# Moving the second GEMM's products one unit later in the pinned order of a fused attention and feed-forward kernel

## The chip, the cores and the metric

The kernel runs on one core of a Trainium2 chip. The metric is the device time of one execution in microseconds. Three runs of the kernel before took 962.63, 962.66 and 961.5 us, a median of 962.63 us.

## What is computed

The input is q, k and v of 8 batches, 8 heads, 576 positions and 64 channels, in float32. Two attentions are added: one over sequences shortened by a mean over four positions, and a local one in which each position sees itself and three neighbours on either side. The sum becomes the rows `x` of a feed-forward layer with 4608 rows, 512 inputs and 2048 hidden values:

```python
    x = np.ascontiguousarray(attn_out.transpose(0, 2, 1, 3)).reshape(B * S, H * D)
    h = x @ w_in
    r = np.maximum(h, 0.0)
    g = s * (r * r) + b
    return (g @ w_out).astype(np.float32)
```

## The kernel before

**Tiles.** The rows are cut into 18 tiles `t` of 256, the hidden values into 8 parts `p` of 256. A block is one pair (t, p); `order` lists the 144 blocks. From t = 3 on, where this study plays, the blocks come in plain order, eight to a row tile, so that block 8t + p is (t, p). To keep float32 precision every operand is split in a high and a low part (`xh`, `xl`, `gh`, `gl`), and each product is made of three matmuls.

**A block's work.** `products1` (L631) multiplies `w_in` with `x`: 24 matmuls of 256 columns into one PSUM bank `ph`. It yields after 3, 12 and 24 of them, so it is given out in parts of 3, 9 and 12. Then ScalarE works in place on `ph`: relu (L646) and square (L647), and casts it to `gh` (L648). VectorE subtracts `gh` from `ph` and writes `gl` (L653), after which the bank is free. `products2` (L712 to L714) multiplies `g` with `w_out`: four units of three matmuls of 512 columns, two units for the upper 128 rows (m = 0, into one bank `po`), two for the lower (m = 1, into another). The sums over the eight parts p stay in these two banks.

**Eviction.** With part p = 7 a row tile is done. After the second unit of that block `evict_half` (L686) scales the m = 0 bank into `os` on VectorE, after the fourth unit the m = 1 bank, and SyncE sends each with a DMA (L689). From t = 3 on all row tiles use the same two banks (0 and 1), so the next tile's first unit, which starts a new sum in bank 0, must wait until the m = 0 eviction has read it.

**Buffers.** Even blocks use bank 4 for `ph`, odd ones bank 6. There are three pairs of `gh` and `gl`, so the cast of block n must wait for the last unit of block n - 3.

**The order of the work.** An order written out by hand (`PLAN`) runs the first 28 blocks, with their w_out products, among the start of the attention. Behind it a loop takes two blocks at a time, `st` (even) and `st + 1`. In it `products("G", n)` gives out n parts of w_in's products and `products("H", n)` n units of w_out's, and every matmul of both is chained to the one before, so that TensorE meets them in exactly the order of the text. An iteration is: 3 products of block st, one unit, 21 products of block st, one unit, 24 products of block st + 1, six units. `finish` issues the relu, square, cast and subtraction of a block. In the iteration of st = 28 (`BEGIN`) no unit is given out, and the loop ends with eight units, so that the units trail: before the change the six units of an iteration are units 2 and 3 of block st - 2 and all four of block st - 1.

**The attention beside it.** `advance` and `split` issue steps of the attention of later batches and the split of the next row tile of `x` (L612, L613). The local attention multiplies q with shifted k on GpSimd (L537), sums on VectorE (L539), takes a softmax (L542 to L550), multiplies v by the weights on VectorE (L558) and adds on GpSimd or VectorE (L559). Its loads `lqk` and `lv` (L530, L532) go through SyncE's queue, as do those of the other attention (L154) and the stores of `os`. A scheduler with a simulated timeline places the attention's instructions on all engines, and the eviction, the subtraction and the casts with them. Each engine then runs its own list in order.

Of the kernel before, what the change touches and what calls it, by code (L numbers as in the profile page):

```python
# [20 lines left out]
B, H, S, D = 8, 8, 576, 64  # L21
# [65 lines left out]
def attention_ffn_kernel(ctx, tc, qk, vw_in, vr_in, vdm, qkn, vn, w_in, w_out, s_in, b_in, out):  # L87
# [706 lines left out]
    BEGIN = 28  # L794
# [66 lines left out]
    @contextlib.contextmanager  # L861
    def behind_plan():

        traced = nc.cur_bb.bb.instructions
        last = traced[-1]
        yield
        start = next(k for k in reversed(range(len(traced))) if traced[k] is last) + 1
        for i in traced[start:]:
            if i.engine in ENGINES:
                tc.add_manual_dep(  # L870
                    i, tail[i.engine].name,
                    mybir.DependencyInfo(
                        mybir.DependencyClass.NoSync, mybir.DependencyReason.DATA),
                    reason="behind_plan")
# [3 lines left out]
    def products(kind, count):  # L878

        nonlocal chain_end  # L880
        for _ in range(count):
            traced = nc.cur_bb.bb.instructions
            last = traced[-1]
            next(streams[kind])
            start = next(k for k in reversed(range(len(traced))) if traced[k] is last) + 1
            for i in traced[start:]:
                if i.engine == nc.tensor.engine:
                    tc.add_manual_dep(
                        i, chain_end.name,
                        mybir.DependencyInfo(  # L890
                            mybir.DependencyClass.NoSync, mybir.DependencyReason.DATA),
                        reason="products")
                    chain_end = i

    def finish(st):
        with tc.high_priority():
            next(streams["R"])
            next(streams["V"])
        advance(st + 0.5)
# [32 lines left out]
    def advance(st):  # L932
        nonlocal done
        while done < target(st):
            with tc.high_priority(offset=300 if done < NY[1] else 60 if done < NY[1] + NY[2] else 0):
                if next(gen, "end") == "end":
                    break
            done += 1
# [3 lines left out]
    def split(st):  # L942
        if order[st] in splits:
            split_x(splits[order[st]])

    for st in range(BEGIN, len(order), 2):
        begun = st > BEGIN
        with behind_plan() if st < BEGIN + 10 else contextlib.nullcontext():
            products("G", 1)
            products("H", 1 * begun)  # L950
            products("G", 2)
            finish(st)
            products("H", 1 * begun)
            advance(st + 1)
            split(st)
            products("G", 3)
            finish(st + 1)
            products("H", 6 * begun)
            advance(st + 2)
            split(st + 1)  # L960
    products("H", 8)


def _layout(q, k, v):
# [59 lines left out]
```

## Time and profile before

| | |
|---|---|
| median of three runs | 962.63 us (961.5 to 962.66) |
| profiled execution | 959.7 us |
| its span, first to last instruction | 957.9 us |
| TensorE busy | 924.6 us, 97% of the span |
| VectorE, ScalarE, GpSimd busy | 645.2, 478.2 and 412.9 us |
| granted TensorE clock, mean | 0.989 |

In the rows of the views PE is TensorE, PEld its weight loads, DVE VectorE, ACT ScalarE, POOL GpSimd, and SPq the queue of SyncE, which issues the DMAs. A row of the waits has the engine and line that waited, who ended the wait, and then microseconds in total, number of times and the longest. A row of the timeline has a start, a duration (from the first start to the last end where several instructions are merged, xN) and, in brackets, the idle time of the engine just before it and who ended it. A row of the chain has a start, a length and the work; consecutive matmuls stand there from start to start. A row of the windows has the stretch, its length, each engine's busy time and number of instructions, the granted clock, the busy share of the DMA engines and GB/s.

### The profile page before, as it was taken

To read this page: it belongs to the slowest core of one execution; us is meant where nothing else is said; L and a number is where in the kernel's file an instruction comes from. 1 tells how busy PE (TensorE), PEld (TensorE's weight loads), DVE (VectorE), ACT (ScalarE), POOL (GpSimd) and SP (SyncE) were. 2 spreads that over 40 slices of the span, in tenths; PEclk is the share of its full clock that TensorE was granted. 3 is DMA by queue.
4 is the path that set the end of the run, shared out by engine and by line. 5 is a ranking of instruction groups with operands and counts; after the bars stand their busy time and mean duration, and the time that the engine had idled before them with its cause. 6 is when DMAs were issued, how large, how long until landed. Compare 5 with 4: busy or idle time off the path is not lost.

```text
span 957.9 us, 18429 instructions
## 1 busy us (share of the span) xinstructions
PE 924.6 (97%) x7316; PEld 831.1 (87%) x7316; DVE 645.2 (67%) x1134; ACT 478.2 (50%) x1133; POOL 412.9 (43%) x440
## 2 busy tenths in 40 slices
PE   6699999999999999999999999999999999999998
PEld 5588888888889989898999899889898999999997
DVE  9999999844688879787878797787877421211121
ACT  7977775466553636354544454544434333332332
POOL 6401130010587776767676768676776200000000
PEclk9699999999999999999999999999999999999999
DMA  9755413223232323323232323232311000000000
GB/s 327 264 169 179 144 47 114 71 71 102 90 107 96 110 89 108 97 91 111 83 106 81 123 79 126 80 113 91 114 54 43 1 23 1 23 1 23 1 23 22
DMA packets 32022, 86.25 MB, mean 90 GB/s; under 512 B 3520, under 2 KB 8128, under 8 KB 31936
## 3 DMA queue, kind: packets, MB, share of 16 engines
q1 hardware_dynamic: 31936, 85.08, 27.2%
q8 instruction: 57, 0.93, 0.4%
q14 instruction: 29, 0.24, 0.1%
HBM read 75.63 MB, written 9.44 MB: 89 GB/s over the span
## 4 chain that ended last, share of the span: by engine, by line
PE 54%; DVE 18%; POOL 17%; issue 5%; ACT 3%; DMA 2%; DVEq 0%; POOLq 0%; ACTq 0%
PE ph L631 24%; PE po L712 8%; POOL pr L537 8%; PE po L713 8%; PE po L714 8%; POOL acc L559 6%; DVE pv L558 3%; DVE acc L559 2%; DVE gl L653 1%; DVE st L539 1%; DVE bias L669 1%; PE sa L342 1%; DMA lqk<-in_qkn_dram 1%; PE ol L479 1%; DVE es L272 1%
## 5 line engine op out<-in xcount | busy, mean ns | idle before, releaser
L631 PE MATMUL ph<-xh,wi 128*128 128x256 f32 x2176 | 414.0, 280 | 1.6 <-DVE gl L653 1.6
L631 PEld LDWEIGHTS ph<-xh,wi 128*128 128x128 f32 x2176 | 345.2, 189 | 10.7 <-DVE gl L653 2.7
L631 PE MATMUL ph<-xl,wi 128*128 128x256 f32 x1152 | 321.6, 279 | 0.0
L537 POOL TENSOR_TENSOR pr<-lqk 128x576 f32<-128x576 f32 x140 | 206.4, 1495 | 77.0 <-DMA lqk<-in_qkn_dram 53.7
L631 PEld LDWEIGHTS ph<-xl,wi 128*128 128x128 f32 x1152 | 217.4, 189 | 7.3 <-DVE xl L771 0.2
L646 ACT ACTIVATE ph<-ph 128x512 f32<-128x512 f32 x144 | 83.9, 582 | 235.1 <-PE ph L631 227.1
L712 PE MATMUL po<-wo,gh 128*128 128x512 f32 x416 | 166.3, 400 | 4.6 <-DVE os L686 4.5
L713 PE MATMUL po<-wo,gh 128*128 128x512 f32 x416 | 164.0, 394 | 0.0
L714 PE MATMUL po<-wo,gl 128*128 128x512 f32 x416 | 162.8, 391 | 0.8 <-DVE gl L653 0.7
L653 DVE TENSOR_TENSOR gl<-ph,gh 128x512 fp32r<-128x512 f32 x104 | 71.0, 683 | 105.4 <-ACT gh L648 105.0
L539 DVE TENSOR_REDUCE st<-pr 128x9 f32<-128x576 f32 x140 | 106.2, 759 | 48.4 <-POOL pr L537 45.9
L559 POOL TENSOR_TENSOR acc<-acc,pv 128x576 f32<-128x576 f32 x80 | 115.0, 1437 | 54.0 <-DVE pv L558 31.5
L558 DVE TENSOR_TENSOR pv<-lv,st 128x576 f32<-128x576 f32 x120 | 87.3, 745 | 32.4 <-POOL acc L559 32.1
L312 POOL TENSOR_TENSOR dq<-vt 80x64 f32<-80x64 f32 x58 | 20.7, 368 | 174.5 <-PE up L383 173.3
L714 PEld LDWEIGHTS po<-wo,gl 128*128 128x128 f32 x416 | 78.1, 188 | 18.9 <-DVE gl L653 2.1
L712 PEld LDWEIGHTS po<-wo,gh 128*128 128x128 f32 x416 | 78.1, 188 | 18.6 <-DVE os L686 4.4
L713 PEld LDWEIGHTS po<-wo,gh 128*128 128x128 f32 x416 | 78.3, 188 | 11.1 <-issue 0.2
L647 ACT ACTIVATE ph<-ph 128x512 f32<-128x512 f32 x144 | 83.8, 582 | 3.7
L712 PE MATMUL po<-wo,gb 128*128 128x512 f32 x160 | 63.3, 396 | 3.5 <-DVE os L686 3.5
L648 ACT CAST gh<-ph 128x512 fp32r<-128x512 f32 x104 | 61.0, 587 | 9.5 <-PE po L713 6.7
L653 DVE TENSOR_TENSOR gb<-ph,gb 128x512 fp32r<-128x512 f32 x40 | 27.3, 682 | 53.9 <-ACT gb L648 53.9
L713 PE MATMUL po<-wo,gb 128*128 128x512 f32 x160 | 62.9, 393 | 0.0
(158 smaller groups left out, 1243.2 us busy)
## 6 DMA issues: line engine op xcount, KB each, us to landing
tqk<-in_qk_dram SPq DMA_DIRECT2D x30, 584.0 KB, 3.7
lqk<-in_qkn_dram SPq DMA_DIRECT2D x20, 768.0 KB, 4.6
lv<-in_vn_dram SPq DMA_DIRECT2D x20, 480.0 KB, 3.3
out_dram<-os SPq DMA_DIRECT2D x34, 256.0 KB, 2.3
wst<-in_moe_w_in_dram SPq DMA_DIRECT2D x7, 1024.0 KB, 5.9
wst<-in_moe_w_out_dram SPq DMA_DIRECT2D x7, 1024.0 KB, 4.9
tvd<-in_vdm_dram SPq DMA_DIRECT2D x29, 160.0 KB, 2.4
tvr<-in_vr_dram SPq DMA_DIRECT2D x29, 128.0 KB, 2.2
```

Source lines behind the costliest of these rows:

```text
L537: nc.gpsimd.tensor_tensor(pr, lqk[:, 0:CH], lqk[:, CH + o : 2 * CH + o], ALU.mult)
L539: nc.vector.tensor_reduce(ls[:, :, o], pr, AX.X, ALU.add)
L558: nc.vector.tensor_tensor(pv, lv[:, o : o + CH], w, ALU.mult)
L559: (nc.vector if o % 3 == 1 else nc.gpsimd).tensor_tensor(acc[:, :, h], acc[:, :, h], pv, ALU.add)
L631: nc.tensor.matmul(ph[:, j], wi[p][:, s, k, f], xk[:, k], start=k == 0 and s == 0 and xk is xh, stop=k == NK - 1 and s == 1)
L646: nc.scalar.activation(ph, ph, AF.Relu)
L647: nc.scalar.activation(ph, ph, AF.Square)
L648: nc.scalar.copy(gh, ph)
L653: nc.vector.tensor_tensor(gl, acc.pop((t, p)), gh.bitcast(F32), ALU.subtract)
L712: nc.tensor.matmul(po[m], gh[:, j, ms], wo[p][:, 0, j], start=first, stop=False)
L713: nc.tensor.matmul(po[m], gh[:, j, ms], wo[p][:, 1, j], start=False, stop=False)
L714: nc.tensor.matmul(po[m], gl[:, j, ms], wo[p][:, 0, j], start=False, stop=last)
```

## The change

One unit of w_out's products less is given out ahead of the 21 products in the iteration of st = 30, the first that gives out any, and one more behind the loop. From then on the stream of units is one unit later against the text of the loop: the unit ahead of the 21 products is the fourth of the block before, the unit behind them the first of block st - 2, and the six behind block st + 1 are units 1, 2 and 3 of block st - 2 and units 0, 1 and 2 of block st - 1. At the end of a row tile the fourth unit of its last block, and the m = 1 eviction that is issued with it, move from the end of one iteration into the next, and the first unit of the next row tile moves from in front of the 21 products to behind them. The number of products and of every other instruction is the same.

```diff
@@ -947,7 +947,7 @@
         begun = st > BEGIN
         with behind_plan() if st < BEGIN + 10 else contextlib.nullcontext():
             products("G", 1)
-            products("H", 1 * begun)
+            products("H", 1 * (st > BEGIN + 2))
             products("G", 2)
             finish(st)
             products("H", 1 * begun)
@@ -958,7 +958,7 @@
             products("H", 6 * begun)
             advance(st + 2)
             split(st + 1)
-    products("H", 8)
+    products("H", 9)
```

## The prediction

> **What bounds the kernel now.** I read the page first, for the engine that fills the span, and then the busy time by stage.
>
> ```profile
> span 957.9 us, 18429 instructions
> PE 924.6 (97%) x7316; PEld 831.1 (87%) x7316; DVE 645.2 (67%) x1134; ACT 478.2 (50%) x1133; POOL 412.9 (43%) x440
> PE 54%; DVE 18%; POOL 17%; issue 5%; ACT 3%; DMA 2%; DVEq 0%; POOLq 0%; ACTq 0%
> 262.00:742.00 480.00, 470.88 (x3184) 428.35 (x3184) 383.66 (x684) 229.10 (x587) 346.64 (x321) 1.00 0.30 96
> 742.00:957.00 215.00, 212.08 (x1381) 192.05 (x1379) 45.60 (x69) 69.79 (x119) 5.75 (x4) 1.00 0.04 13
> ```
>
> TensorE fills the span, yet the chain gives it only 54%: a third of the chain runs over VectorE (DVE) and GpSimd (POOL). From 262 to 742 us, where the loop runs beside the attention, TensorE idles 9.1 us of 480. The granted clock is 1.00 there. Who ends that idle time is in the waits of TensorE over the whole span, and what a free iteration takes is in the chain of waits of the last stage:
>
> ```profile
> PE po L712 <- DVE os L686: 8.0, 8, 1.9
> PE ph L631 <- DVE gl L653: 1.6, 3, 1.0
> ...
> 785.30 2.38 PE ph L631 x21
> 788.38 2.72 PE ph L631 x24
> 796.26 2.38 PE ph L631 x21
> ```
>
> Eight times the first unit of a row tile waits for the eviction of the same bank, 8.0 us in all, the longest 1.9. It is the change's target. In the last stage an iteration takes 796.26 - 785.30 = 10.96 us without any wait; the 48 w_in products at 2.72 / 24 = 0.113 us leave 5.52 us for 24 w_out products, 0.23 each, so a unit is 0.69 us. The longest of the eight waits, in the timelines of TensorE and of VectorE:
>
> ```profile
> 734.21 0.39 PE L714 MATMUL po<-wo,gl 128*128 128x512 f32 x1
> ...
> 736.40 0.41 PE L370 MATMUL tr<-ident,pd 96*64 96x96 f32 x3
> 738.71 0.50 PE L712 MATMUL po<-wo,gb 128*128 128x512 f32 x1 [1.90 <-DVE os L686]
> 739.05 0.39 PE L713 MATMUL po<-wo,gb 128*128 128x512 f32 x1
> ```
>
> ```profile
> 735.27 0.76 DVE L539 TENSOR_REDUCE st<-pr 128x9 f32<-128x576 f32 x1 [1.32 <-POOL pr L537]
> 736.65 0.76 DVE L539 TENSOR_REDUCE st<-pr 128x9 f32<-128x576 f32 x1 [0.62 <-POOL pr L537]
> 737.32 0.68 DVE L653 TENSOR_TENSOR gl<-ph,gh 128x512 fp32r<-128x512 f32 x1
> 737.92 0.74 DVE L686 SCALAR_TENSOR_TENSOR os<-po,sb_s,bias 128x512 f32<-128x512 f32 x1
> 738.58 0.75 DVE L539 TENSOR_REDUCE st<-pr 128x9 f32<-128x576 f32 x1
> 739.24 0.74 DVE L686 SCALAR_TENSOR_TENSOR os<-po,sb_s,bias 128x512 f32<-128x512 f32 x1
> ```
>
> The bank was complete at 734.21 + 0.39 = 734.60, but the eviction started at 737.92. It stood in VectorE's list behind two reductions that waited 1.32 and 0.62 us for GpSimd, and behind a subtraction. So the lateness is the attention's, passed on through VectorE's order.
>
> **The unit that moves behind the 21 products.** Between the unit that completes m = 0 and the next tile's first unit lie now two units and 3 w_in products, 2 x 0.69 + 3 x 0.113 = 1.72 us. After the change the same two units and 24 products lie there: 4.10 us. The margin grows by the 21 products, 2.38 us, more than the longest wait of 1.9. Taken alone, all eight waits go. The work of TensorE stays the same.
>
> A wait costs more than its idle column. After the third transposition, which starts at about 736.56 (0.41 us for three, one of them 0.25 by the group row below), the next start would have been at 736.65; it came at 738.71, 2.06 later, and the matmul behind it followed after 0.34 instead of 0.23. That is 2.17 where the column has 1.90: 0.27 more, and for eight waits 8 x 0.27 = 2.2. So the most that can be had is 8.0 + 2.2 = 10.2 us.
>
> ```profile
> L370 PE MATMUL tr<-ident,pd 96*64 96x96 f32 x87 | 11.9, 246 | 0.3 <-DVE pl L447 0.3
> ```
>
> The Trainium skill, in Perfetto Trace Analysis, section "Tensor Engine Instruction (MATMUL, LD_WEIGHTS)", says that a matmul's end in a profile is computed from its size and not observed. Whoever took those ends at face value would stop at 8.0 us; the starts above, 2.17 against 1.90, agree with the page, so I count by starts.
>
> **How much VectorE lets through.** A TensorE that no longer waits runs ahead, and what is late next is the subtraction that frees the `ph` bank for the block after next. Two row tiles show it, in the timelines of TensorE and then of VectorE:
>
> ```profile
> 633.99 0.38 PE L631 MATMUL ph<-xh,wi 128*128 128x256 f32 x1 [0.34 <-DVE gl L653]
> ...
> 636.34 0.50 PE L712 MATMUL po<-wo,gh 128*128 128x512 f32 x1 [1.18 <-DVE os L686]
> ...
> 685.21 0.38 PE L631 MATMUL ph<-xh,wi 128*128 128x256 f32 x1 [0.24 <-DVE gl L653]
> ```
>
> ```profile
> 633.28 0.66 DVE L653 TENSOR_TENSOR gl<-ph,gh 128x512 fp32r<-128x512 f32 x1
> ```
>
> The subtraction ends at 633.94 and TensorE goes on at 633.99. There, and at 685.21 one row tile on, it has no margin against `gl`: if VectorE kept its times of before, any lead won earlier would be lost there. That is the lower bound: after 685.21 the longest eviction wait, at 738.71, is still to come, and at the last one TensorE can be no more than the 21 products ahead of what it was, because the eviction ends when it ended. Gain 2.4 us.
>
> But VectorE does follow TensorE in part. Its waits in this stage, then GpSimd's for loads and ScalarE's for TensorE:
>
> ```profile
> DVE st L539 <- POOL pr L537: 45.7, 51, 2.2
> DVE pv L558 <- POOL acc L559: 31.2, 21, 3.1
> ...
> DVE gl L653 <- ACT gh L648: 3.3, 5, 1.2
> ...
> DVE gb L653 <- ACT gb L648: 1.0, 1, 1.0
> ```
>
> ```profile
> POOL pr L537 <- DMA lqk<-in_qkn_dram: 47.2, 14, 6.1
> ```
>
> ```profile
> ACT gh L648 <- PE po L713: 3.7, 3, 1.4
> ACT gb L648 <- PE po L714: 2.4, 6, 1.2
> ```
>
> VectorE waits 3.3 + 1.0 = 4.3 us for casts, which TensorE paces; an earlier TensorE shortens these waits, and the attention moves forward by up to 4.3 us. The rest of its waits, 45.7 and 31.2, are with GpSimd and don't move with TensorE. So TensorE can end 2.4 + 4.3 = 6.7 us earlier.
>
> **The cast that comes later.** The cast of block st + 1 waits for the last unit of block st - 2. That was the second unit behind block st + 1's products and is now the third: 0.69 us later. ScalarE and everything queued behind the cast on it wait with it, and VectorE's `gl` behind those. Today 9 casts of the stage wait, 6.1 us. TensorE itself has room: from the end of an odd block's products to the next use of its bank lie 18 + 3 + 3 w_out and 24 w_in products, 24 x 0.23 + 2.72 = 8.24 us. But where VectorE had caught up and waits for that cast, it gets 0.69 us less of TensorE's lead. What counts is the last such place before the last eviction wait, so once 0.69. Bounds are 0 (the lead covers it) and 0.69 for each of the ten row tiles in the stage, 6.9. I take 0.69, because one recovered eviction wait, 1.0 + 0.27 us in the mean, already gives a lead above that, and every later catch-up finds it. For even blocks the last unit of block st - 3 now ends ahead of the 21 products, 2.38 us before the cast can be wanted: nothing.
>
> **What else moves.** The m = 1 eviction is issued after the first 3 products of the next iteration. It needs its unit 3 x 0.113 + 0.69 = 1.0 us later than now. Its reader is the third unit of the new block, behind 21 + 24 products and two units, 6.5 us, so it costs nothing on TensorE. Its DMA and that of m = 0 stand in SyncE's queue, where loads wait that GpSimd needs (47.2 us above):
>
> ```profile
> 687.53 0.37 SPq L689 DMA_DIRECT2D out_dram<-os  x1
> 689.53 0.33 SPq L530 DMA_DIRECT2D lqk<-in_qkn_dram  x1
> 689.91 0.42 SPq L689 DMA_DIRECT2D out_dram<-os  x1
> ```
>
> The `lqk` load stands between the two stores, 2.0 us behind the first. m = 0 is now in place one unit, 0.69 us, later, which the 2.0 cover; m = 1 goes further back. Nothing, as long as the order stays; if the second store were put ahead of the load, each load would come about 1 us later. GpSimd's queue holds nothing of what is moved.
>
> At the loop's start three products fewer stand in front, and three more behind the loop: 0 in sum, as long as block 31 doesn't wait for its bank 0.69 us earlier.
>
> ```profile
> 260.30 0.38 PE L631 MATMUL ph<-xh,wi 128*128 128x256 f32 x1 [1.04 <-DVE gl L653]
> 265.00 0.37 PE L631 MATMUL ph<-xh,wi 128*128 128x256 f32 x1
> ...
> 262.22 0.68 DVE L653 TENSOR_TENSOR gb<-ph,gb 128x512 fp32r<-128x512 f32 x1
> ```
>
> Its bank is free at 262.90 and wanted at 265.00, so 1.4 us remain. The 1.04 us of block 30 stand ahead of all that is changed, and stay.
>
> **Sum.** 2.4 + 4.3 - 0.69 = 6.0 us gained. The profiled execution took 959.7 us (span 957.9 and 1.8 around it) and would take 953.7. The median of the runs is 2.9 us above the profiled one; 962.63 - 6.0 = 956.6 us.
>
> **Rivals.** (1) TensorE keeps the whole: the attention follows it fully, 10.2 us, 952.4. For it: the subtraction has margin again in the middle of row tiles. Against: the two places without margin. (2) VectorE's times stay: 2.4 us, 960.2. For it: 77 of its waits' microseconds are GpSimd's. Against: the 4.3 us. (3) The change doesn't do what it says: the scheduler, which orders VectorE by its own timeline, puts the m = 0 eviction, now ready a unit later, behind more of the attention; two reductions with their waits, as those above from 735.27 - 1.32 to 737.32, take 3.4 us and eat the 2.38. The waits stay at 8.0 and the time at 962.6. (4) Slower, by the later cast: 0.69 us of delay in each of ten row tiles, 6.9, against 2.4 gained, is 4.5 more: 967.1. It decides from the point where a row tile's delay exceeds what VectorE now idles for casts in it (4.3 / 10 = 0.43), if TensorE's lead stays under 0.69 there. The Trainium skill, in TensorE: Matmul & The Clock Gate, section "Architectural detail", calls the queues of ScalarE and VectorE strictly first in, first out; by that rule all behind the cast is held, which would be this rival; the eviction at 737.92 shows the order for VectorE.
>
> **Chances.** The forecast 0.45, whole gain 0.15, VectorE's times kept 0.17, no effect 0.13, slower 0.10. A measurement of this kernel can tell about 0.2%, 1.9 us, from no change. Faster by more: the first three, 0.77; within it 0.13; slower 0.10. The range runs from the whole gain, 952.4, to just short of no effect, 962.0, and leaves out the slower case and half of the one without effect.
>
> **What would show it.** The wait of `po` for `os` falls from 8.0 us to under 1; the wait of `ph` for `gl` grows from 1.6 to 2 or 4 at the first even block of a row tile; VectorE's waits for casts shrink by less than 4.3; ScalarE's casts wait more for `po`; the last stage keeps 10.96 us an iteration. It is wrong if the eviction wait stays, or if it goes and the stage with the attention is no shorter.

## The result, and the profile after

The changed kernel took 953.48 us in the median (951.22 to 953.71) against 962.07 us before: ratio 0.9906 [0.9888, 0.9924]. Repeated beside 23 runs of the kernel before, it took 952.93 us (six runs, 950.91 to 955.37) against 962.15: 0.9911 [0.9891, 0.9931]. So 8.6 to 9.2 us are gained; the forecast was 6.0. Here and below a ratio is that of a kernel's times to those of the kernel before, run beside it, with a 95% interval in brackets.

The first profiled execution (1026.8 us) ran at a granted clock of only 0.844, and two of e5's (1148 us, one of them its profile) at about 0.75, so these times are left out, the rows of the changed kernel are from the repeat, e1_again (953.1 us), and none are shown of e5.

The profiled executions are 6.6 us apart in their spans, less than the medians, because that of before (959.7 us) is quicker than its median. The page of the changed kernel, and its busy time in the stage with the attention:

```profile
span 951.3 us, 18420 instructions
PE 922.6 (97%) x7316; PEld 832.7 (88%) x7316; DVE 648.3 (68%) x1134; ACT 474.3 (50%) x1133; POOL 411.5 (43%) x440
```

```profile
262.00:742.00 480.00, 477.02 (x3232) 436.53 (x3231) 391.11 (x690) 229.96 (x596) 346.23 (x323) 1.00 0.30 96
```

In the stage with the attention TensorE idled 480 - 470.88 = 9.1 us before and 480 - 477.02 = 3.0 us now. These 6.1 us are most of the difference of the spans. TensorE's busy time fell by 2.0 us besides (924.6 to 922.6) for the same matmuls, close to the 2.2 us that the prediction counted on top of the idle column; outside this stage its idle time is 1.5 us longer, which takes off again nearly as much. What is left of TensorE's waits from 262 to 970 us, and the chain of waits of the last stage:

```profile
PE sa L342 <- DVE x L573: 2.6, 4, 0.8
PE ph L631 <- DVE gb L653: 0.3, 1, 0.3
```

```profile
898.57 2.38 PE ph L631 x21
901.65 2.72 PE ph L631 x24
909.53 2.38 PE ph L631 x21
```

The waits of `po` for the eviction, 8.0 us before, are gone. An iteration of the last stage takes 909.53 - 898.57 = 10.96 us, as before. The waits of VectorE and then of ScalarE in the stage with the attention:

```profile
DVE st L539 <- POOL pr L537: 39.8, 50, 1.6
DVE pv L558 <- POOL acc L559: 22.4, 14, 3.4
...
DVE gl L653 <- ACT gh L648: 2.1, 4, 1.6
DVE gb L653 <- ACT gb L648: 0.8, 4, 0.3
```

```profile
ACT gh L648 <- PE po L713: 7.9, 12, 0.7
...
ACT gb L648 <- PE po L714: 6.4, 7, 0.9
```

VectorE's waits for GpSimd, which the prediction held fixed, fell from 45.7 + 31.2 to 39.8 + 22.4 us. Its waits for casts fell from 4.3 to 2.9 only. One more wait for GpSimd, that of `acc`, grew from 3.6 to 7.1 us, so that VectorE's waits for GpSimd fell by 11.2 us in all.

**The eviction is as late as before.** The end of row tile 9, in the timelines of TensorE and of VectorE:

```profile
629.84 0.39 PE L714 MATMUL po<-wo,gl 128*128 128x512 f32 x1
...
634.78 0.40 PE L712 MATMUL po<-wo,gh 128*128 128x512 f32 x1
```

```profile
630.54 0.76 DVE L539 TENSOR_REDUCE st<-pr 128x9 f32<-128x576 f32 x1 [0.90 <-POOL pr L537]
631.90 0.75 DVE L323 TENSOR_REDUCE qd<-tqk 128x144 f32<-128x576 f32 x1 [0.60 <-DMA tqk<-in_qk_dram]
632.58 0.68 DVE L653 TENSOR_TENSOR gb<-ph,gb 128x512 fp32r<-128x512 f32 x1
633.17 0.74 DVE L686 SCALAR_TENSOR_TENSOR os<-po,sb_s,bias 128x512 f32<-128x512 f32 x1
```

The m = 0 bank is complete at 629.84 + 0.39 = 630.23. The eviction starts 2.94 us later, behind two reductions that waited 0.90 and 0.60 us, and a subtraction. It ends at 633.91. The next tile's first product comes at 634.78, without a wait. With the 1.72 us of margin of before it would have waited here, since 2.94 us pass before the eviction even starts. Nothing made the eviction quicker; the 21 products cover it.

### The profile page after: what moved, and what is told of

It reads as the page before. It is cut to its first block, busy times and chain, and to the rows that moved or that the text cites. A ratio compares the mean times of both kernels' runs of the same rounds, so it can differ in the third digit from the quotient of the medians.

```text
span 1025.0 us, 18420 instructions
## 1 busy us (share of the span) xinstructions
PE 1002.2 (98%) x7316; PEld 885.1 (86%) x7316; DVE 658.1 (64%) x1134; ACT 474.7 (46%) x1133; POOL 408.9 (40%) x440
## 4 chain that ended last, share of the span: by engine, by line
PE 92%; DVE 5%; ACT 1%; issue 1%; POOL 0%; DVEq 0%; POOLq 0%; ACTq 0%
PE ph L631 41%; PE po L712 14%; PE po L713 14%; PE po L714 14%; PE sa L342 2%; PE up L383 1%; PE ot L569 1%; PE ol L479 1%; PE tr L370 1%; PE up L381 1%; DVE bias L669 1%; PE sl L436 1%; PE tp L368 1%; DVE es L272 0%; DVE es L269 0%
## 5 line engine op out<-in xcount | busy, mean ns | idle before, releaser
L631 PE MATMUL ph<-xh,wi 128*128 128x256 f32 x2176 | 451.4, 293 | 0.7 <-DVE gl L653 0.7
L631 PEld LDWEIGHTS ph<-xh,wi 128*128 128x128 f32 x2176 | 364.8, 196 | 11.9 <-DVE gl L653 0.9
L631 PE MATMUL ph<-xl,wi 128*128 128x256 f32 x1152 | 337.0, 293 | 0.9 <-DVE xl L771 0.9
L631 PEld LDWEIGHTS ph<-xl,wi 128*128 128x128 f32 x1152 | 226.0, 196 | 11.6 <-DVE xl L771 1.1
L537 POOL TENSOR_TENSOR pr<-lqk 128x576 f32<-128x576 f32 x140 | 198.0, 1433 | 71.0 <-DMA lqk<-in_qkn_dram 50.2
L712 PE MATMUL po<-wo,gh 128*128 128x512 f32 x416 | 175.2, 421 | 0.0
L713 PE MATMUL po<-wo,gh 128*128 128x512 f32 x416 | 174.3, 419 | 0.0
L714 PE MATMUL po<-wo,gl 128*128 128x512 f32 x416 | 173.7, 418 | 0.4 <-DVE gl L653 0.3
L539 DVE TENSOR_REDUCE st<-pr 128x9 f32<-128x576 f32 x140 | 105.9, 756 | 20.5 <-POOL pr L537 17.4
L712 PEld LDWEIGHTS po<-wo,gh 128*128 128x128 f32 x416 | 80.6, 194 | 17.6 <-issue 0.2
L713 PEld LDWEIGHTS po<-wo,gh 128*128 128x128 f32 x416 | 80.8, 194 | 15.7 <-issue 0.3
L713 PE MATMUL po<-wo,gb 128*128 128x512 f32 x160 | 66.9, 418 | 0.0
L714 PE MATMUL po<-wo,gb 128*128 128x512 f32 x160 | 66.7, 417 | 0.0
```

The costliest lines, as they stand in the source:

```text
L537: nc.gpsimd.tensor_tensor(pr, lqk[:, 0:CH], lqk[:, CH + o : 2 * CH + o], ALU.mult)
L539: nc.vector.tensor_reduce(ls[:, :, o], pr, AX.X, ALU.add)
L631: nc.tensor.matmul(ph[:, j], wi[p][:, s, k, f], xk[:, k], start=k == 0 and s == 0 and xk is xh, stop=k == NK - 1 and s == 1)
L712: nc.tensor.matmul(po[m], gh[:, j, ms], wo[p][:, 0, j], start=first, stop=False)
L713: nc.tensor.matmul(po[m], gh[:, j, ms], wo[p][:, 1, j], start=False, stop=False)
L714: nc.tensor.matmul(po[m], gl[:, j, ms], wo[p][:, 0, j], start=False, stop=last)
```

## The experiments

Two theories, called M and S in the texts written ahead of the runs. **Cover** (M): the gain is the 21 products in front of the bank's next use, and VectorE follows TensorE by its cast waits, as predicted. **Lists** (S): the cover is not enough, because a second wait comes up behind the eviction's; the gain needs what the scheduler made of the rest, above all where it put the attention's matmuls on TensorE. Comparing each engine's whole list in the two kernels, 355 of 1134 places differ on VectorE, 341 of 1036 on ScalarE, 54 of 436 on GpSimd and 36 of 204 on SyncE, though the diff moves products alone.

### e1_again: the changed kernel once more

> The changed kernel as it is, once more, for a profile at the full clock. Theory M (the 21 products between a row tile's evictions and the next tile's first unit cover the eviction's lateness): 7 to 10 us under the kernel before; the wait of po for os falls from 8.0 us to under 1, the wait of ph for gl may grow from 1.6 to at most 4. Theory S (the gain is from another order of the attention, which the scheduler made anew): the wait of po for os keeps some microseconds, and the gain is in the idle time behind other releasers.

Its times and rows stand above; they are what Cover expected.

### e2, e4: one end of the move alone

e2 moves only the next tile's first unit, behind the 21 products; e4 only the last unit of a block, in front of them.

```diff
e2_half_first
             products("G", 1)
-            products("H", 1 * begun)
             products("G", 2)
             finish(st)
-            products("H", 1 * begun)
+            products("H", 2 * begun)
```

> Only the first half of the change: no unit ahead of the 21 products, two behind them, the six as before (0, 2, 6). The next tile's first unit is behind the 21 products, the last unit stays where it was, and no cast waits longer than before. Theory M: the same margin of 4.10 us, so 7 to 10 us under the kernel before. If the later cast costs something in the changed kernel (the 0.69 us of the prediction), this one is 0.5 to 2 us faster than the changed kernel; if not, within 1 us of it. Theory S: anything, and not tied to the margin.

```diff
e4_half_last
-            products("H", 1 * begun)
+            products("H", begun + (st > BEGIN + 2))
             products("G", 2)
...
-            products("H", 6 * begun)
+            products("H", 5 * begun)
...
-    products("H", 8)
+    products("H", 9)
```

> Only the second half of the change: the last unit of a block and the next block's first both ahead of the 21 products, one unit behind them, five at the end (2, 1, 5). The m = 1 eviction moves as in the changed kernel, the margin of the m = 0 eviction stays 1.72 us, no cast is later. Theory M: waits of po for os near 8 us, time within 2 us of the kernel before. Theory S: may gain as much as the changed kernel.

e2 took 969.85 us, 1.0089 [1.0071, 1.0107], where Cover expected a gain of 7 to 10 us; e4 963.08, 1.0015 [1.0002, 1.0028]. TensorE's waits in e2, then in e4:

```profile
PE ot L569 <- POOL acc L559: 12.1, 9, 1.9
```

```profile
PE po L712 <- DVE os L686: 6.9, 9, 1.2
PE ot L569 <- POOL acc L559: 1.1, 2, 0.8
```

In e2 no wait for the eviction is left, and in its place stand 12.1 us of waits of the transposes `ot`, which bring the attention's result into the layout of `x`, for GpSimd's last addition. This was the first sign of the second gate. Both kernels have a cost of their own, too, seen in the chain of waits of the last stage of e2 and then of e4, where nothing waits:

```profile
906.61 2.83 PE ph L631 x24
913.54 2.83 PE ph L631 x24
917.75 2.36 PE ph L631 x20
```

```profile
908.56 2.48 PE ph L631 x21
911.74 2.72 PE ph L631 x24
919.62 2.48 PE ph L631 x21
```

e2's iteration takes 917.75 - 906.61 = 11.14 us and e4's 919.62 - 908.56 = 11.06, where the kernels before and after have 10.96. Were it so in all 57 iterations, that would be 57 x 0.18 = 10 us and 57 x 0.10 = 5.7 us. The profiles show less: the span without TensorE's idle time behind 262 us is 957.9 - 9.1 = 948.8 us before, 967.4 - 12.1 = 955.3 in e2 and 961.0 - 8.2 = 952.8 in e4, so 6.5 and 4.0 us more. That is most of e2's loss (3.0 us more of waits are the rest in the profile) and more than e4's. So these two say which waits come, but not what half of the change is worth.

### e3: the later cast alone

The next tile's first unit stays ahead of the 21 products; the unit behind them goes to the end, so that the last unit of block st - 2 is the third behind block st + 1, as in the change.

```diff
e3_cast_late
             finish(st)
-            products("H", 1 * begun)
             advance(st + 1)
...
-            products("H", 6 * begun)
+            products("H", 7 * begun)
```

> Only the later cast: one unit ahead of the 21 products, none behind them, seven at the end (1, 0, 7). The margin of the eviction is 1.72 us as before, and the cast of an odd block waits for the third unit behind its products, as in the changed kernel. Theory M: the waits of po for os stay near 8 us and the time within 2 us of the kernel before; if the later cast has a price, it shows here alone, up to 6.9 us slower. Theory S: a new order as well, so it may gain as much as the changed kernel.

959.67 us, 0.998 [0.9965, 0.9996]: not slower. The eviction's wait stays, in TensorE's waits:

```profile
PE po L712 <- DVE os L686: 7.6, 6, 1.9
```

The later cast does reach VectorE: its waits for casts are 6.5 + 3.9 us here against 4.3 before. But the time shows no price, and the rival that made the change 4.5 us slower falls. The predicted 0.69 us is too small to be told in these times, and the scheduler's lists are new in e3 too.

### e7, e8: the stream one unit further, and one unit the other way

```diff
e7_shift2
-            products("H", 1 * begun)
+            products("H", 1 * (st > BEGIN + 2))
...
-            products("H", 1 * begun)
+            products("H", 1 * (st > BEGIN + 2))
...
-    products("H", 8)
+    products("H", 10)
```

> The stream of units one more unit later: 24 + 21 products and two units and more between the m = 0 bank's completion and the next first unit, 6.8 us. Theory M: no wait of po for os, as in the changed kernel, and no more to gain: 951 to 955. The cast of an odd block waits another 0.69 us; if that has a price it is 1 to 3 us slower than the changed kernel.

```diff
e8_shift_m1
-            products("H", 6 * begun)
+            products("H", (6 + (st == BEGIN + 2))*begun)
...
-    products("H", 8)
+    products("H", 7)
```

> The stream of units one unit earlier than in the kernel before: the margin of the eviction is two units, 1.4 us, and the cast of an odd block waits 0.69 us less. Theory M: the waits of po for os grow by about 0.35 us in each of ten row tiles, to 10 to 13 us, and the time to 963 to 968. Theory S: tied to where the transposes fall, not to the margin.

e7: 951.5 us, 0.991 [0.9889, 0.9931], no wait for the eviction left. One unit further gives no more than the change. e8: 960.92 us, 1.0007 [0.9991, 1.0023], with these waits of TensorE for the eviction:

```profile
PE po L712 <- DVE os L686: 7.5, 8, 1.7
```

With less cover the waits should have grown to 10 to 13 us, and the time to 963 to 968 us. They did not (8.0 before). So the wait is not a fixed lateness minus a fixed cover; the lists, made anew for each order, move with it.

### e5, e6: where the transposes stand

In the kernel before, the scheduler puts the nine groups of `ot` inside or at the end of a block's 24 w_in products, at the latest one w_out product behind them. In the changed kernel all nine stand inside the six units, behind 11 to 17 of their w_out products. One group of each, in the timelines of TensorE and GpSimd, first before and then changed:

```profile
603.87 1.20 PE L569 MATMUL ot<-ident,acc 128*128 128x128 f32 x9
```

```profile
600.86 2.95 POOL L559 TENSOR_TENSOR acc<-acc,pv 128x576 f32<-128x576 f32 x2 [1.53 <-DVE acc L559]
```

```profile
604.68 1.14 PE L569 MATMUL ot<-ident,acc 128*128 128x128 f32 x9
```

```profile
599.63 2.96 POOL L559 TENSOR_TENSOR acc<-acc,pv 128x576 f32<-128x576 f32 x2 [1.54 <-DVE acc L559]
```

Before, GpSimd's addition ends at 603.81 and the transposes start at 603.87, 0.06 us behind it. The waits show next to nothing of this (one wait, 0.2 us in the stage), yet TensorE has no room here: in four of the nine groups the start follows the addition by 0.06 us. In the changed kernel the addition ends at 602.59, and 2.1 us remain.

e5 is the changed kernel with the nine groups pinned to their places of before among the w_in products. e6 is the kernel before with the nine groups pinned behind the fourth of the six units. All else the scheduler places anew. The pin ties a transpose to a product of the given order (the excerpt leaves out the branch that looks up the place):

```diff
+                one_, other = ots[pinned[0]], given[kind][at]
+                if EARLY:
+                    one_, other = other, one_
+                tc.add_manual_dep(
+                    one_, other.name,
+                    mybir.DependencyInfo(
+                        mybir.DependencyClass.NoSync, mybir.DependencyReason.DATA),
+                    reason="pin")
```

> The changed kernel with nine of the attention's ten groups of transposes (ot) put back in TensorE's list to the product of w_in where the kernel before has them; in the changed kernel the scheduler put them some 1 to 3 us of products later. Theory M (the margin of the eviction is all that counts): within 2 us of the changed kernel, 952 to 955. Theory S (the new place of the transposes is needed as well, since TensorE without its eviction waits reaches them before GpSimd has finished what they read): waits of ot for acc of about 1 us in each of nine groups, as in the first half alone, 9 to 13 us in all, and a time of 961 to 966.

> The kernel before with those transposes put behind the fourth of the six units, about where the changed kernel has them. Theory M: the waits of po for os stay, 6 to 9 us, and the time within 2 us of the kernel before. Theory S in its strong form (the place of the transposes alone makes the gain): 952 to 956.

e5 took 961.7 us, 1.0017 [0.9998, 1.0037]: with the transposes early, nothing of the gain is left. Whether TensorE then waits at the transposes isn't shown, for want of a profile. e6, without the change, took 952.21 us, 0.9916 [0.9899, 0.9933]: the same as the change. TensorE's waits in e6 (its lines lie 3 to 6 further down), and VectorE's:

```profile
PE po L718 <- DVE os L692: 3.0, 5, 0.9
```

```profile
DVE st L544 <- POOL pr L542: 29.9, 43, 2.2
...
DVE pv L563 <- POOL acc L564: 10.7, 13, 2.2
DVE gl L659 <- ACT gh L654: 10.4, 13, 1.5
...
DVE gb L659 <- ACT gb L654: 6.2, 8, 1.5
```

The eviction, with no more cover than before, is waited for 3.0 us. VectorE now waits 10.4 + 6.2 us for ScalarE's casts, where it was 4.3 us, and 29.9 + 10.7 for GpSimd, where it was 45.7 + 31.2. Since e6's other lists are new as well, the place of the transposes alone isn't shown to make its gain.

### e9 to e12: the products and the lists apart

In these four kernels every engine's list is fixed as data, so that nothing is placed anew: the instructions are numbered in the order of the text by kind (w_in product, w_out product, eviction, other), and each list is tied from one instruction to the next. The traces bear it out: VectorE, ScalarE and GpSimd run their operations in the order of before in e9 and e11 and in that of the changed kernel in e10 and e12. No kernel was run with its own lists fixed, but an iteration of the last stage keeps 10.96 us in e9 and e10.

```diff
+    for engine, wanted in want.items():
+        line = [own[engine][k] for k in wanted]
+        for a, b in zip(line, line[1:]):
+            tc.add_manual_dep(
+                b, a.name,
+                mybir.DependencyInfo(
+                    mybir.DependencyClass.NoSync, mybir.DependencyReason.DATA),
+                reason="lists")
```

| kernel | w_out products | attention's matmuls on TensorE | lists of the other engines | us | ratio to before |
|---|---|---|---|---|---|
| e9 | changed | as before | as before | 957.48 | 0.9962 [0.9949, 0.9976] |
| e10 | before | as changed | as changed | 964.38 | 1.0031 [1.0011, 1.0051] |
| e11 | before | as changed | as before | 993.69 | 1.0336 [1.0314, 1.0358] |
| e12 | before | as before | as changed | 971.68 | 1.0111 [1.0093, 1.0129] |

> The shift of the units alone: the changed kernel with the order of every instruction pinned, on VectorE, ScalarE, GpSimd and SyncE to the kernel before's own lists, and on TensorE the attention's matmuls to the place among the products that they had there. Theory M (the margin): no waits of po for os, 951 to 955. Theory S (the lists that the scheduler made anew): the eviction waits go, but others of 1 us or more at the transposes or at the subtraction take their place, and the time stays within 2 us of the kernel before.

> The opposite: the products of the kernel before, without the shift, and all else in the order of the changed kernel's lists, the attention's matmuls on TensorE too. Theory M: waits of po for os of 6 us or more and the time within 2 us of the kernel before. Theory S: 951 to 955 without the shift; the waits of po for os fall to 4 us or less, though their margin is 1.72 us as before.

> The kernel before, its products and its lists on VectorE, ScalarE, GpSimd and SyncE, and only the attention's matmuls on TensorE moved to where the changed kernel has them among the products. If the place of the transposes on TensorE is what counts (they stand 1 to 3 us of products later): 951 to 956. If the lists of the other engines count: within 2 us of the kernel before, with waits of po for os near 8 us.

> The kernel before with its whole TensorE list, and the lists of the changed kernel on VectorE, ScalarE, GpSimd and SyncE. If the place of the transposes on TensorE counts: within 2 us of the kernel before. If the lists of the other engines count: 951 to 956, and VectorE waits less for GpSimd than the 45.7 + 31.2 us of the kernel before.

e9 is the change as the prediction thought of it, the products moved and all else in its order. It gives 3.7 us, not 9: less than Cover expected, and more than Lists did. TensorE's waits in e9, and the group of transposes shown above, on TensorE and on GpSimd:

```profile
PE ot L827 <- POOL acc L817: 9.0, 9, 1.8
PE ph L896 <- DVE gl L918: 0.3, 1, 0.3
```

```profile
606.37 1.20 PE L827 MATMUL ot<-ident,acc 128*128 128x128 f32 x9 [0.67 <-POOL acc L817]
```

```profile
603.38 2.94 POOL L817 TENSOR_TENSOR acc<-acc,pv 128x576 f32<-128x576 f32 x2 [1.54 <-DVE acc L817]
```

The eviction's 8.0 us are gone and 9.0 us of waits for the transposes have come, one at each of the nine groups. The 0.06 us of before have become a wait: TensorE, held no longer at the eviction, reaches the transposes before GpSimd (ended at 606.32) is done. (e9's profiled execution took 959.1 us, 1.6 more than its median, and only 0.6 less than that of before; so the 3.7 us stand in the times and not in these two profiles.) VectorE's waits for GpSimd in e9 stay as they were:

```profile
DVE st L797 <- POOL pr L795: 46.4, 51, 2.1
DVE pv L816 <- POOL acc L817: 32.6, 19, 3.8
```

The lists of the changed kernel without its products (e10) don't help either, and half of them does harm; none of the times expected for e10, e11 and e12 came true. With the new lists VectorE's two waits for GpSimd fall to 34.1 + 11.6 us in e10, though its products are those of before. TensorE's waits in e10, in e11 and in e12, and one of VectorE in e11:

```profile
PE po L977 <- DVE os L951: 10.0, 10, 2.3
```

```profile
PE po L977 <- DVE os L951: 22.0, 10, 3.7
PE ph L896 <- DVE gl L918: 4.9, 8, 1.1
```

```profile
PE po L977 <- DVE os L951: 13.8, 10, 3.1
PE ot L827 <- POOL acc L817: 3.8, 6, 1.6
```

```profile
DVE x L831 <- PE ot L827: 20.5, 9, 3.7
```

In e11 the transposes come later, but VectorE's list still has the addition that reads them at its place of before. VectorE waits there for TensorE, 20.5 us, and all that stands behind that addition in its list comes later: TensorE's wait for the eviction grows to 22.0 us. The Trainium skill, in TensorE: Matmul & The Clock Gate, section "Architectural detail", calls VectorE's queue strictly first in, first out; e11 agrees with it, at 20.5 us of waits on VectorE and 14.0 more of TensorE's for the eviction than before.

## Why the prediction was right or wrong

**What bounds the kernel, and the cover: right.** The eviction's lateness is the attention's, passed on through VectorE, and the 21 products cover it. The 8.0 us of waits go to nothing in the changed kernel, and in e9, where nothing else moves.

**"How much VectorE lets through": this step failed.** It named the subtraction `gl` as what is late next, and expected TensorE's wait for it to grow from 1.6 to between 2 and 4 us. It did not: over the whole span it is 1.3 us in the changed kernel and 1.4 in e9, and from 262 us on one wait of 0.3. What is late next is the transposes, which wait for GpSimd; e9 shows them at 9.0 us. The prediction does not name them; the waits of before gave them 0.2 us. The two terms of the step fared differently:

- 2.4 us, if all lists keep their order: e9 measures 3.7, and its interval is 2.3 to 4.9 us (0.0024 and 0.0051 of 961.3), so 2.4 lies just inside. The gate that sets it was another.
- 4.3 us, by VectorE's waits for casts: these shrank by 1.4 only, in the changed kernel and, with the old lists, in e9 (to 2.0 + 0.9). "The rest of its waits, 45.7 and 31.2, are with GpSimd and don't move with TensorE" holds as long as the lists stay (46.4 and 32.6 in e9); in the changed kernel they fell by 5.9 and 8.8 us, because the scheduler made other lists, which the sum does not allow for. The attention's last addition on GpSimd ends at 752.8 us before and at 748.2 in the changed kernel, 4.6 us earlier; in e9, with the old lists, it ends at 754.0.

So 953 against the forecast 956.6 is a near hit by luck, for a wrong reason: 3.7 us are the move, and the other 5 the new lists together with it. Not the changed kernel's lists by themselves: with before's products they cost 0.3% (e10). A row tile has two gates, the eviction and the transposes, and the whole gain needs margin at both. The move gives it to the first, the later transposes to the second. e9 has only the first (9.0 us of waits at the transposes) and e10 only the second (10.0 us at the eviction); so much their profiles show. e5, which puts the transposes back, loses the gain; its time alone shows that. The move isn't the only way to open the first gate: e6 makes the same gain without it, with lists in which the eviction is waited for 3.0 us instead of 8.0. The rival in which the scheduler's new order undoes the gain saw the right cause with the wrong sign.

**The later cast: right that it is small.** ScalarE's casts wait 14.3 us instead of 6.1, as foreseen. In e3, where the cast is later and the margin as before, the time is not slower, 0.998; and e9, where with the old lists these casts wait 15.0 + 7.0 us, still gains 3.7. The term's 0.69 us is too small to be confirmed or refused by that.

**The whole gain of 10.2 us,** given 0.15, was closer than the forecast (952.4). It assumed that the attention follows TensorE fully, which e9 does not show: there its last addition comes no earlier. That TensorE's idle time in the stage fell by two thirds has the cause above.

**Open.** Which of the hundreds of changed places on VectorE, ScalarE and GpSimd make the attention 4.6 us quicker was not taken apart, nor why e6's lists make the eviction less late. Why e9 gains 3.7 us in its times with as much waiting in its profile as before (9.3 us in the stage against 9.1) is open too; the profiled execution, 1.6 us above the median, explains it only in part. No version was found that beats the change: by their ratios e6 (0.9916) and e7 (0.991) can't be told from it (0.9911).

## What to carry to other kernels

When a wait is to be covered, list the places behind it where an engine arrives just as its data does (here 0.06 us behind the addition): the waits view gave them next to nothing, and they took over as soon as the engine was earlier; the term to compute is the margin at the next such place, not the wait removed. Where a scheduler places the rest, a two-line edit is a new set of lists: tell the two apart by fixing the lists, and try pinning a late consumer (here nine groups of transposes) before moving the products, since that gave the same gain (0.9916) with lists made anew around it. The lists of the engines belong together: TensorE's new places of the attention's matmuls under the old lists of the others cost 3.4%, the others' new lists under TensorE's old one 1.1%.

## What the runs showed of the hardware

The start-to-start time of w_in products differs with the run of w_out products in front. Behind three w_out products 21 of them take 2.38 us and 24 take 2.72, 113 ns each; behind six or eighteen (e2) 24 take 2.83, and behind six in e4 21 take 2.48, 118 ns each, over the whole run of products. With them goes an iteration of the last stage that is 0.18 us longer in e2 and 0.10 in e4. The cause was not tested.
